# Merged gate lists carried to their sorting lanes by TensorE instead of four DMAs, with sort steps and first-tile gates moved between rounds

## The chip, the cores and the metric

The kernel runs on one core of a Trainium2 chip. The metric is the device time of the program in microseconds (us). The kernel before was run 9 times: median 312.01 us, lowest 308.48, highest 314.27. The engines are named as in the profile: PE is TensorE's matrix product, PEld its weight load, DVE is VectorE, ACT is ScalarE, POOL is GpSimd, SP is SyncE, which here only issues DMAs.

## What is computed

Two layers follow each other. The first is attention with a choice of key chunks; the second is a mixture of experts with a capacity.

```python
# attention: q, k, v are (4, 8, 768, 64); 24 chunks of 32 keys
ub = sum(max(q * k_min, q * k_max))            # bound of each chunk, for each query
top_chunks = argsort(where(causal, ub, -1e9))[..., -6:]
attn = softmax(scale * q @ k.T, only in the 6 chunks and causal)
x = (attn @ v) as (3072 tokens, 512)
# experts: 8 of them, each takes at most 80 tokens
expert = argmax(x @ w_gate); gate = its softmax weight
for e in range(8):
    tok = the 80 tokens of e with the highest gates
    out[tok] = gate[tok] * (relu(x[tok] @ w1[e]) @ w2[e])   # all other rows 0
```

So for each expert the 80 highest gates among 3072 tokens have to be known before the expert's tokens can be fetched.

## The kernel before

**Rounds.** The 32 pairs of batch and head are taken in eight groups of four (g = 0 to 7); two groups make a batch. The 768 queries of a group are three tiles of 256 (t = 0, 1, 2). A round `rd` is one pair of key blocks for one tile: a group has 1 + 2 + 3 = 6 rounds, and there are N = 48. Everything is in one hand-written order (`manual_schedule`): each engine runs its instructions in the order in which the Python code issues them, and waits only for semaphores.

**A round** issues, in this order: `rows` (for the tile that ended four rounds ago: TensorE transposes, L564, and the normalised rows of x by DVE, L565; at the second group of a batch the store of x to DRAM, L571), `scales` (tile that ended three rounds ago: L542, L544, L550, and in the second group of a batch `best`, which finds each token's expert, L581 to L603), `score` (L459, L463), `gate_rows` (L530, L534), `exps` (ACT, L474, four per round; on diagonal blocks a mask on POOL, L479), `sum_pairs` (POOL, L503), the queue `late` (`flush`), transposes of the next group's q and k on DVE (`step`, L262, L279), then `pace(rd)` **sort steps**, then the product with v for the round before (`value`, L492), its denominators (`denom`, L517), and in the round r = 3 of a group the bounds of the next group's chunks (`bound_all`, L390; `rank_all`, L402 to L410). At the end of the round stands `gates` (L616 to L640 on DVE): it turns a tile's winning logits into gates, writes them to `gmask`, and queues eight small POOL operations (`columns`, L623 to L650) that the next flush issues.

**The sort.** In a batch's second group, the gates of a tile go to `gmask`. Four generators then find the top 80 of each expert, eight at a time: one step is a MAX8 (L661) and a match-and-replace (L663) on DVE. `lanes1` sorts columns 0 to 7 of `gmask` in 64 lanes, `lanes_mid` merges them with columns 8 to 11 in 32 lanes, `lanes2` sorts columns 12 to 15 and merges (L703, result `M3`, 32 lanes of 80 values: four lists for each of eight experts). `lanes3` sorts what is left: two sets of eight lanes, at partitions 0 and 32, each with two of the four lists and one more column (16 or 17). To get there, `lanes2` moves the four lists by four DMAs from SBUF to SBUF on SP's queue (L707). Each generator starts with a TensorE transpose (`turned`, L669) into a PSUM tile of the pool `misc`, which has two buffers for all its tiles, and an ACT copy (`copied`, L674). Each list takes 10 steps. The generators run one after the other; `merges` holds them, and a generator is added three rounds after the round in which its tile ended. `pace(rd)` says how many steps a round issues; the step that ends a generator counts too.

**What needs the result.** In round 44 `freeze` transposes the eight thresholds to all partitions (L734, `ps_tau`), compares all gates with them (L745, L746), counts with TensorE (`ps_cum`, L755 to L759), and builds the old tokens' seats (L763 to L775, `ps_old`). It must be past the last sort step. `ps_tau` stands on TensorE's queue ahead of `value(43)`.

The steps of a round, and the end of `lanes2`:

```python
for _ in range(pace(rd)):
    if merges and next(merges[0], merges) is merges:
        merges.pop(0)
...
if 1 <= rd < N:
    value(rd - 1)
```

Of the kernel before, what the change touches and what calls it, by code (L numbers as in the profile page):

```python
# [8 lines left out]
F32 = mybir.dt.float32  # L9
# [12 lines left out]
NB = 4  # L22
# [3 lines left out]
NEXP = 8  # L26
DFF = 1024
CAP = 80
NPRE = 5
QBLK = SEQ // P  # L30
# [6 lines left out]
def kernel(  # L37
# [11 lines left out]
    nc = tc.nc  # L49
# [16 lines left out]
    ident_f32 = cpool.tile([P, P], F32, name="ident_f32")  # L66
# [136 lines left out]
    with tc.tile_pool(name="small", bufs=2) as small, \  # L203
# [11 lines left out]
        def misc(shape, dtype, name):  # L215
            return psM.tile(shape, dtype, space=bass.MemoryType.PSUM, tag="misc", name=name)
# [341 lines left out]
        def rows(g, t):  # L558
            b, gi = divmod(g, 2)
            npt, rec = nps.pop((g, t)), recs.pop((g, t))  # L560
            ps_xn = misc([P, 2, 2, P], F32, "ps_xn")
            for a in range(2):
                for j in range(2):
                    nc.tensor.transpose(ps_xn[:, j, a, :], npt[:, a, j * P:(j + 1) * P], ident_f32[:])  # L564
            nc.vector.tensor_tensor(  # L565
                out=xbuf[(b, t)][:, :, P * gi:P * (gi + 1)].bitcast(
                    BF16).rearrange("p j (k d) -> p j k d", d=HEAD_D),
                in0=ps_xn[:].rearrange("p j a (r d) -> p j (a r) d", d=HEAD_D),
                in1=rec[:, :, :, None].to_broadcast([P, 2, 4, HEAD_D]), op=ALU.mult)
            if gi == 1:  # L570
                nc.sync.dma_start(out=x_dram_v[:, QBLK * b + 2 * t:QBLK * b + 2 * t + 2, :],  # L571
                                  in_=xbuf[(b, t)][:])

        picked = {}

# [97 lines left out]
        def copied(dst, src):  # L673
            nc.scalar.activation(out=dst, in_=src, func=mybir.ActivationFunctionType.Copy)  # L674
# [17 lines left out]

        def lanes_mid():
            copied(S2[:, CAP:], turned(8, 4)[:])
            nc.gpsimd.memset(S3, -1.0)
            yield from sort_lanes(S2, L2)

        def lanes2():
            S, L = cand[0][32:64, 208:208 + P], cand[0][32:64, 416:416 + CAP]
            copied(S, turned(12, 4)[:])  # L700
            yield from sort_lanes(S, L)
            reversed_copy(back, L)
            nc.vector.tensor_tensor(out=M3, in0=L2, in1=back, op=ALU.max)  # L703
            yield
            for i in range(4):
                w, n = divmod(i, 2)
                nc.sync.dma_start(  # L707
                    out=cand[0][32 * n:32 * n + NEXP, 496 + CAP * w:496 + CAP * (w + 1)],
                    in_=cand[1][NEXP * i:NEXP * (i + 1), CAP:2 * CAP])

        def lanes3():
            for n in range(2):
# [298 lines left out]

        N = len(rounds)
        merges = []
        pace = lambda rd: {42: 6, 43: 6}.get(rd, ((0, 5, 3, 2, 1, 1), (0, 5, 1, 1, 1, 0))[rd // 6 % 2][rd % 6])
        steps_of = {1: ["K0"], 2: ["K1", "Q0"], 3: ["Q1"], 6: ["K0", "K1"], 7: ["Q0"], 8: ["Q1"]}
        for g in range(2, NQUAD - 1):
            steps_of.update({6 * g - 1: ["K0"], 6 * g: ["K1"], 6 * g + 1: ["Q0"], 6 * g + 2: ["Q1"]})
# [3 lines left out]
        with tc.manual_schedule(engines=set(mybir.EngineType) - {mybir.EngineType.Unassigned}):  # L1021
            first, others = slice(0, 2), slice(2, QBLK)
            load(0, k4, "kn", first)
            load(0, q4, "qn", first, nc.scalar)
            nc.scalar.activation(out=minus1[:], in_=crow[:], func=mybir.ActivationFunctionType.Exp,
                                 scale=1e-3)
            load(0, k4, "kn", others)
            load(0, q4, "qn", others)
            load_v(0, first)
            nc.sync.dma_start(out=wg_sb[:], in_=moe_w_gate.rearrange("(t r) e -> r t e", r=P))  # L1030
            load_v(0, others)
            load_k(1)
            load_q(1)
            load_v(1)
            idle(24)
            u = prep(0)
            units = [u]
            u["K"](0)
            u["Q"](0)
            flush()  # L1040
            u["bound"](1, 2)
            idle(5)
            u["K"](1)
            u["rank"](1, 2)
            u["Q"](1)
            build = {0: build_constants, 1: build_projection, 3: build_selection, 4: build_ties}
            for rd in range(N + 1):
                g, r = divmod(rd, 6)
                if r == 1 and 1 <= g < NQUAD - 1:
                    load_v(g + 1)  # L1050
                if r == (1 if g else 3) and g + 2 < NQUAD:
                    load_k(g + 2)
                if r == (3 if g else 4) and g + 2 < NQUAD:
                    load_q(g + 2)
                if 16 <= rd < 40 and rd % 2 == 0:
                    zero_fill((rd - 16) // 2)
                if rd - 4 in ends:
                    rows(*ends[rd - 4])
                if rd - 3 in ends:
                    eg, et = ends[rd - 3]  # L1060
                    scales(eg, et)
                ps_S = score(rd) if rd < N else None
                if rd - 2 in ends:
                    gate_rows(*ends[rd - 2])
                if rd < N:
                    exps(rd, ps_S)
                    if summed(rd):
                        sum_pairs(rd)
                flush()
                if rd - 3 in ends and eg == NQUAD - 1:  # L1070
                    gates(eg // 2, et)
                if rd in build:
                    build[rd]()
                if r in (2, 4) and 1 <= g <= NPRE or r == 2 and g == NPRE + 1:
                    load_whole(g - 1, r // 2 - 1)
                late_weights(rd)
                if rd == 0:
                    units[0]["bound"](2, 4)
                    units[0]["K"](2)
                    units[0]["rank"](2, 4)  # L1080
                    units[0]["Q"](2)
                elif rd == 1:
                    units[0]["bound"](4, 6)
                    units[0]["rank"](4, 6)
                for kind, f in steps_of.get(rd, []):
                    if (kind, f) == ("K", "0"):
                        units.append(prep(len(units)))
                    units[-1]["step"](kind, int(f))
                u = units[min(g + 1, NQUAD - 1)] if len(units) > g + 1 else None
                at = 3 if g else 4  # L1090
# [3 lines that stand above are left out]
                if (rd, 0) in frozen:  # L1094
                    next(fz, None)
                if rd == N - 1:
                    turn_new(0)
                if 1 <= rd < N:
                    value(rd - 1)
                    if r == at and g + 1 < NQUAD:  # L1100
                        u["bound_all"]()
                    if r == 5 and g + 1 < NQUAD:
                        u["unselect"]()
                    denom(rd - 1)
                    del Es[rd - 1]
                    gl, t, i, pr, n = rounds[rd - 1]
                    if i == n - 1:
                        evacuate(gl, t)
                        ends[rd - 1] = (gl, t)
                if r == at and g + 1 < NQUAD:  # L1110
                    u["rank_all"]()
                flush(bulk)
                if rd == N - 1:
                    weigh0()
                    turn_new(1)
                if (rd, 1) in frozen:
                    assert not merges
                    next(fz, None)
                if rd - 3 in ends:
                    eg, et = ends[rd - 3]  # L1120
                    if eg % 2 == 1 and eg < NQUAD - 1:
                        gates(eg // 2, et)
                    make = {(3, 0): lanes1, (3, 2): lanes_mid, (5, 1): lanes2, (5, 2): lanes3}.get(ends[rd - 3])
                    if make:
                        merges.append(make())
            last = (NQUAD - 1, 2)
            weigh1()
            denom(N - 1)
            value(N - 1)
            evacuate(*last)  # L1130
            weigh1_own()
            gate_rows(*last)
            held_back.pop(0)()
            scales(*last)
            held_back.pop(0)()
            weigh1_sum()
            gates(NB - 1, 2)
            flush()
            rows(*last)
            idle(10)  # L1140
            turn_new(2)
            weigh2()
# [108 lines left out]
```

## Time and profile before

| | |
|---|---|
| median of 9 runs | 312.01 us |
| the profiled execution | 313.38 us, of which the span from first to last instruction is 311.7 us |
| mean granted TensorE clock in it | 0.942 |
| PE busy | 265.0 us, 85% of the span |
| DVE busy | 201.4 us, 65% |
| ACT busy | 153.8 us, 49% |
| POOL busy | 196.5 us, 63% |
| the four DMAs of L707 | issued from 210.86 to 214.03 us |
| sort steps (L661, L663) on DVE | first at 120.7 us, last at 228.0 us |

A matmul line of the timeline merges many instructions, with the time from the first start to the last end. Square brackets at the end of a timeline line give how long the engine stood still before it and for whom; "issue" there means that the profile shows nobody that it waited for. PEclk is the clock that TensorE was granted, 1.00 being full speed; in the trace it is 1.00 or 0.50 in stretches of 3.4 us.

### The profile page before, as it was taken

Reading aid. Unit: us, or ns where it says so; the run is one execution under the profiler, and the core shown is the slowest. Engines: PE = TensorE matmul, PEld = TensorE weight load, DVE = VectorE, ACT = ScalarE, POOL = GpSimd, SP = SyncE. Lnnn points to the kernel's source line nnn. Section 1 sums busy time; section 2 is a strip of 40 time slices with the busy share of each in tenths; the row PEclk is TensorE's granted clock in tenths of the full one; section 3 lists DMA queues with packets and bytes.
Section 4 is the critical chain, followed back from the end, with each engine's and each line's share of the span. In section 5 each row is a group of like instructions: output and inputs, shape, how many; then the busy total and the mean of one; then the engine's idle time right before and its main releaser. Section 6 shows DMA issues by size and latency. Waiting matters only on the chain.

```text
span 311.7 us, 12157 instructions
## 1 busy us (share of the span) xinstructions
PE 265.0 (85%) x5018; PEld 158.8 (51%) x5018; DVE 201.4 (65%) x747; ACT 153.8 (49%) x351; POOL 196.5 (63%) x398
## 2 busy tenths in 40 slices
PE   8769789989979997989999798799556878779992
PEld 3326456546646664556666455455324544327760
DVE  4849279369747546998997597941868574742431
ACT  1643948727936863765686268526602334422120
POOL 8294886958967875896788579729913220237232
PEclk9999999999999999999999899979859589969998
DMA  7887706979999999999999996719998100102211
GB/s 173 173 181 147 147 3 140 191 148 171 200 220 247 212 252 267 208 211 234 274 205 248 270 214 184 130 44 137 201 208 136 36 3 34 34 23 67 63 59 40
DMA packets 59303, 47.80 MB, mean 153 GB/s; under 512 B 27910, under 2 KB 51590, under 8 KB 59248
## 3 DMA queue, kind: packets, MB, share of 16 engines
q1 hardware_dynamic: 45392, 28.10, 37.5%
q0 software_dynamic: 13536, 18.67, 34.7%
q8 instruction: 39, 0.64, 0.9%
q10 hardware_dynamic: 320, 0.26, 0.3%
q14 instruction: 16, 0.13, 0.1%
HBM read 53.10 MB, written 10.76 MB: 205 GB/s over the span
## 4 chain that ended last, share of the span: by engine, by line
PE 55%; DVE 18%; issue 11%; POOL 4%; DMA 4%; ACT 3%; SPq 2%; POOLq 1%; ACTq 0%; DVEq 0%
PE ps_num L492 21%; PE ps_den L517 8%; PE ps_u L390 7%; PE ps_S L459 6%; PE ps_xn L564 4%; PE ps_den L530 3%; DVE cand L663 3%; PE ps_S L463 2%; DVE cand L661 2%; POOL X L1154 2%; POOL out_dram L1196 2%; PE ps_dT L542 2%; DMA cand<-cand 2%; DVE cand L770 2%; ACT E L474 2%
## 5 line engine op out<-in xcount | busy, mean ns | idle before, releaser
L474 ACT ACTIVATE E<-ps_S 128x384 f32<-128x384 f32 (+1 forms) x192 | 88.7, 554 | 46.7 <-PE ps_S L463 46.7
L492 PE MATMUL ps_num<-E,vn 128*32 128x256 f32 (+1 forms) x1536 | 94.6, 366 | 3.3 <-issue 3.3
L503 POOL TENSOR_TENSOR both<-E 128x256 f32<-128x256 f32 x92 | 64.6, 732 | 23.3 <-ACT E L474 23.2
L492 PEld LDWEIGHTS ps_num<-E,vn 128*32 128x32 f32 x1536 | 50.8, 112 | 34.0 <-issue 10.8
L479 POOL TENSOR_SCALAR_AFFINE_SELECT E<-E 128x256 f32<-128x256 f32 x96 | 41.4, 461 | 34.3 <-ACT E L474 34.3
L459 PE MATMUL ps_S<-QB,KB 32*128 32x256 bf16 (+1 forms) x768 | 35.4, 264 | 2.4 <-ACT E L474 1.7
L534 ACT ACTIVATE DSB<-ps_den 128x256 f32<-128x256 f32 x24 | 9.2, 385 | 42.3 <-PE ps_den L530 38.7
L463 PE MATMUL ps_S<-PENT,ind 32*128 32x256 bf16 (+1 forms) x384 | 25.1, 258 | 2.5 <-DVE PENT L377 2.5
L517 PE MATMUL ps_den<-E,ones 128*32 128x256 f32 (+1 forms) x400 | 23.4, 339 | 2.2 <-issue 2.2
L459 PEld LDWEIGHTS <-KB 32*128 32x128 bf16 x768 | 17.2, 94 | 15.2 <-issue 11.9
L287 POOL CAST KB<-kT 128x768 bf16<-128x768 f32 (+1 forms) x18 | 24.1, 1343 | 0.0
L565 DVE TENSOR_TENSOR x_nat<-ps_xn,rec 128x512 bf16<-128x512 f32 x24 | 16.5, 686 | 11.2 <-PE ps_xn L564 8.1
L517 PE MATMUL ps_den<-both,ones 128*32 128x256 f32 x184 | 19.5, 402 | 0.0
L402 DVE STREAM_TRANSPOSE ub<-ps_u 128x160 f32<-128x160 f32 x28 | 7.4, 318 | 18.6 <-PE ps_u L390 18.6
L296 ACT ACTIVATE qp<-qT 128x640 f32<-128x640 f32 (+2 forms) x20 | 12.8, 647 | 12.4 <-DVE qT L262 12.3
L517 PEld LDWEIGHTS ps_den<-E,ones 128*32 128x32 f32 x400 | 13.2, 112 | 10.8 <-issue 5.9
L661 DVE MAX8 cand<-cand 64x8 f32<-64x128 f32 (+3 forms) x40 | 13.7, 342 | 6.9 <-DMA cand<-cand 4.2
L262 DVE STREAM_TRANSPOSE kT<-kn 128x768 f32<-128x768 f32 (+1 forms) x17 | 15.6, 919 | 3.7 <-DMA kn<-in_k_dram 3.6
L564 PE MATMUL ps_xn<-ident_f,npt 128*128 128x128 f32 x96 | 16.6, 298 | 1.6 <-DVE sm L616 1.0
L523 ACT ACTIVATE npt<-ps_num 128x512 f32<-128x512 f32 x24 | 14.8, 616 | 5.0 <-PE ps_num L492 5.0
L279 DVE TENSOR_REDUCE KMM<-kT 128x24 f32<-128x768 f32 (+1 forms) x20 | 15.8, 791 | 1.5 <-PE ps_u L355 0.9
L1196 POOL DMA_INDIRECT out_dram<-Y,sidx x8 | 7.4, 922 | 13.9 <-DVE Y L1194 13.9
(238 smaller groups left out, 459.2 us busy)
## 6 DMA issues: line engine op xcount, KB each, us to landing
w<-in_moe_w_dram POOLq DMA_DIRECT2D x11, 1024.0 KB, 10.8
out_dram<-zero_tile SPq DMA_DIRECT2D x12, 512.0 KB, 12.3
kn<-in_k_dram SPq DMA_DIRECT2D x28, 192.0 KB, 5.0
qn<-in_q_dram SPq DMA_DIRECT2D x28, 192.0 KB, 7.0
vn<-in_v_dram SPq DMA_DIRECT2D x28, 192.0 KB, 5.2
x_dram<-x_nat SPq DMA_DIRECT2D x12, 257.0 KB, 5.5
kn<-in_moe_w_dram POOLq DMA_DIRECT2D x1, 768.0 KB, 7.9
qn<-in_moe_w_dram POOLq DMA_DIRECT2D x1, 768.0 KB, 12.6
```

What stands on the lines that cost most here:

```text
L287: nc.gpsimd.tensor_copy(out=straight(KB[s][:, f, ts]), in_=natural(kT[:, f, ts]))
L390: nc.tensor.matmul(out=tiles[h][32 * j:32 * (j + 1), :, :], lhsT=KMM[s][rs, w, f, :], rhs=x[rs, j], start=(w == 0 and f == 0), stop=(w == ...
L459: nc.tensor.matmul(out=ps_S[h][:, m, 0:wid], lhsT=KB[s][rs, w, keys], rhs=QB[s][rs, w, q0:q0 + wid], start=(w == 0), stop=False, skip_grou ...
L463: nc.tensor.matmul(out=ps_S[h][:, m, lo - q0:wid], lhsT=ind[rs, keys], rhs=PENT[s][rs, lo - NFULL:q0 + wid - NFULL], start=False, stop=Tru ...
L474: nc.scalar.activation(out=E[:].rearrange("p m q -> p (m q)")[:, 0:last], in_=ps_S[h][:].rearrange("p m q -> p (m q)")[:, 0:last], func=my ...
L479: nc.gpsimd.affine_select(out=diag, in_=diag, compare_op=ALU.is_ge, fill=0.0, base=0, pattern=[[0, 2], [1, 4], [4, CHUNK]], channel_multip ...
L492: nc.tensor.matmul(out=NUM[q0:q0 + 32, a, c0:THIRD], lhsT=nats[(g, "vn")][:, kb, 2 * a + r, 32 * f:32 * (f + 1)], rhs=Es[rd][2 * a + r][:, ...
L503: nc.gpsimd.tensor_tensor(out=both[:], in0=E[:, 0, :], in1=E[:, 1, :], op=ALU.add)
L517: nc.tensor.matmul(out=dn[32 * h:32 * (h + 1), c0:THIRD], lhsT=ones32[:], rhs=src, start=(i == 0 and m == 0), stop=False, skip_group_check ...
L564: nc.tensor.transpose(ps_xn[:, j, a, :], npt[:, a, j * P:(j + 1) * P], ident_f32[:])
L565: nc.vector.tensor_tensor(out=xbuf[(b, t)][:, :, P * gi:P * (gi + 1)].bitcast(BF16).rearrange("p j (k d) -> p j k d", d=HEAD_D), in0=ps_xn ...
L661: nc.vector.max(out=top, in_=src)
```

## The change

Four edits. (1) `lanes2` ends with four TensorE products with shifted 32 columns of the identity instead of four DMAs; they write the four lists to a PSUM tile `ps_m` of pool `misc` at partitions 0 and 32, and one ACT copy of 40x160 brings them to the lanes of `lanes3`. The POOL memset of those lanes shrinks to the columns that are not copied. (2) For the first tile of a group (t = 0) the gates, and with them the start of `lanes1`, come four rounds after its end instead of three: from the end of round 6g+3, behind `rank_all`, to the end of round 6g+4. (3) Since the stored rows hold the gate, the store of x for such a tile moves behind its gates (except in the last batch). (4) `pace` is set anew.

```diff
-            if gi == 1:
-                nc.sync.dma_start(out=x_dram_v[:, QBLK * b + 2 * t:QBLK * b + 2 * t + 2, :],
-                                  in_=xbuf[(b, t)][:])
+            if gi == 1 and (t or b == NB - 1):
+                store(b, t)
+
+        def store(b, t):
+            nc.sync.dma_start(out=x_dram_v[:, QBLK * b + 2 * t:QBLK * b + 2 * t + 2, :],
+                              in_=xbuf[(b, t)][:])
...
         def lanes_mid():
             copied(S2[:, CAP:], turned(8, 4)[:])
-            nc.gpsimd.memset(S3, -1.0)
+            nc.gpsimd.memset(S3[:, 2 * CAP:], -1.0)
...
             nc.vector.tensor_tensor(out=M3, in0=L2, in1=back, op=ALU.max)
             yield
+            ps_m = misc([64, 2 * CAP], F32, "ps_m")
             for i in range(4):
                 w, n = divmod(i, 2)
-                nc.sync.dma_start(
-                    out=cand[0][32 * n:32 * n + NEXP, 496 + CAP * w:496 + CAP * (w + 1)],
-                    in_=cand[1][NEXP * i:NEXP * (i + 1), CAP:2 * CAP])
+                nc.tensor.matmul(out=ps_m[32 * n:32 * (n + 1), CAP * w:CAP * (w + 1)],
+                                 lhsT=ident_f32[0:32, NEXP * i:NEXP * i + 32], rhs=M3, start=True, stop=True,
+                                 skip_group_check=True)
+            copied(S3[:, 0:2 * CAP], ps_m[0:40, :])
...
-        pace = lambda rd: {42: 6, 43: 6}.get(rd, ((0, 5, 3, 2, 1, 1), (0, 5, 1, 1, 1, 0))[rd // 6 % 2][rd % 6])
+        pace = lambda rd: {23: 1, 40: 3, 41: 4, 42: 4, 43: 4}.get(
+            rd, ((0, 4, 1, 3, 0, 1), (0, 4, 4, 3, 0, 1))[rd // 6 % 2][rd % 6])
...
-                if rd - 3 in ends:
-                    eg, et = ends[rd - 3]
-                    if eg % 2 == 1 and eg < NQUAD - 1:
+                for d in (3, 4):
+                    eg, et = ends.get(rd - d, (0, 0))
+                    if eg % 2 == 1 and eg < NQUAD - 1 and (et == 0) == (d == 4):
                         gates(eg // 2, et)
-                    make = {(3, 0): lanes1, (3, 2): lanes_mid, (5, 1): lanes2, (5, 2): lanes3}.get(ends[rd - 3])
-                    if make:
-                        merges.append(make())
+                        if et == 0:
+                            store(eg // 2, et)
+                        make = {(3, 0): lanes1, (3, 2): lanes_mid, (5, 1): lanes2,
+                                (5, 2): lanes3}.get((eg, et))
+                        if make:
+                            merges.append(make())
```

Counted out, the steps fall like this (the step that ends a generator included; rounds without a step left out):

| rounds | before | after |
|---|---|---|
| 22 to 27 | 1 in 22, then 5, 3, 2 in 25 to 27 | 1 in 23, then 4, 1, 3 in 25 to 27 |
| 28 to 35 | 1, 1 in 28 and 29; 5, 1, 1, 1 in 31 to 34 | 1 in 29; 4, 4, 3 in 31 to 33; 1 in 35 |
| 37 to 40 | 5, 3, 2, 1 | 4, 1, 3, 3 |
| 41 to 43 | 1, 6, 6 | 4, 4, 4 |

`M3` is ready with the step of round 41 before, and with the last step of round 40 after. The move to the lanes of `lanes3` is the first step of round 42 before, and the first step of round 41 after.

## Prediction

> **What bounds the kernel now.** I read the wait view first, for TensorE: who stood still longest, and for whom. From the answer sorted by time:
>
> ```profile
> PE ps_tau L734 <- DVE cand L717: 7.2, 1, 7.2
> ...
> DVE cand L661 <- DMA cand<-cand: 4.2, 1, 4.2
> ```
>
> The columns are total us, times, longest. TensorE's longest wait in the run is the threshold transpose of round 44, which waits for the end of the last sort. The sort in turn waited for the four DMAs. The timeline of each engine gives the times. DVE, SP and TensorE:
>
> ```profile
> 210.56 0.23 DVE L703 TENSOR_TENSOR cand<-cand,cand 32x80 f32<-32x80 f32 x1
> ...
> 218.67 0.45 DVE L661 MAX8 cand<-cand 40x8 f32<-40x288 f32 x1 [4.16 <-DMA cand<-cand]
> ```
> ```profile
> 210.86 3.17 SPq L707 DMA_DIRECT2D cand<-cand  x4
> ```
> ```profile
> 221.48 0.63 PE L530 MATMUL ps_den<-npt,wgx 128*32 128x256 f32 x4
> 229.27 0.27 PE L734 MATMUL ps_tau<-ident_f,cand 8*128 8x8 f32 x1 [7.16 <-DVE cand L717]
> 229.47 3.64 PE L492 MATMUL ps_num<-E,vn 128*32 128x256 f32 x32
> 232.88 1.08 PE L517 MATMUL ps_den<-both,ones 128*32 128x256 f32 x8
> ```
>
> M3 is ready at 210.79, its lanes only at 218.67: 3.17 us of issue, then 5.14 us (in the chain of waits) until the last transfer lands. Ten steps follow without a gap to 229.21. So the chain is DVE, SP, DMA, DVE, and TensorE stands. The last two lines show a second cost: 32 products take 3.64 us, where the same line takes 1.93 at 214.77. The windows view says why (columns: PE, PEld, DVE, ACT, POOL busy, PEclk, DMA share, GB/s):
>
> ```profile
> 118.50:121.90 3.40, 1.89 (x32) 1.07 (x36) 2.59 (x12) 1.88 (x6) 2.56 (x9) 1.00 1.08 256
> ...
> 173.10:176.50 3.40, 1.41 (x28) 0.78 (x22) 2.39 (x12) 1.78 (x5) 2.47 (x8) 1.00 1.10 248
> 176.50:179.90 3.40, 3.40 (x46) 1.48 (x42) 1.19 (x6) 0.00 (x0) 1.85 (x6) 0.50 1.07 328
> ...
> 229.30:234.50 5.20, 5.20 (x45) 2.35 (x46) 1.91 (x6) 0.00 (x0) 0.00 (x0) 0.50 1.16 208
> ```
>
> After stretches in which TensorE was busy 35 to 43% (1.18 of 3.40 at 200.4, 1.41 at 173.1) the next 3.4 us were granted half speed; after one at 56% (1.89 at 118.5) they were not. A half stretch full of work costs 1.7 us.
>
> **Edit 1 with the new steps of rounds 40 to 43.** Removed: four DMAs, whose path from M3 to the first step is 7.88 us. Added: four products, a copy, and an earlier place. DVE has room in round 40: it stands 3.73 us ahead of L544 at 209.80. Its three steps there (0.70, a lone MAX8 of 0.28, then L684 and L703 of 0.53) take about 1.5 us from 205.79, so M3 is ready near 207.3. The four products come in round 41 behind `score`, at 210.46, and wait for nothing. No row has this form; the two transposes of L669 at 214.21 take 0.63 together, so four small ones lie between 0.3 and 1.3, and I take 0.45, nearest to that row.
>
> Now a new wait. TensorE's queue then holds the transposes of columns 16 and 17 and `value(40)`. `misc` has two buffers: the second transpose takes the buffer of `ps_m`, which the ACT copy must empty. That copy is queued behind the four exponentials of round 41 (210.62 to 212.68 on ACT). Copies of the L674 rows take 0.27, so: copy to 212.95, second transpose 213.0 to 213.3, its copy to 213.6, first step of the last sort near **213.7 instead of 218.67**. TensorE stands from 211.2 to 213.0, 1.8 us, and `value(40)` with all behind it starts at 213.3 instead of 210.46: 2.84 later, less 0.56 because the transposes no longer stand in round 42 (214.21 to 214.77). So TensorE comes to `ps_tau` at 222.11 + 2.28 = 224.4.
>
> DVE's last sort is 218.67 to 229.21, 10.54 us, now cut by the x row of round 42 (0.61): 213.7 + 10.54 + 0.61 = 224.85. Both arrive nearly together; `ps_tau` runs near 225.0 instead of 229.27, **4.3 earlier**.
>
> **The clock behind it.** TensorE no longer stands 7 us, so `value(43)` and its denominators run at full speed: 3.64 - 1.93 and 1.08 - 0.61 are 2.18, of which the overlap of the two lines leaves 2.1. That stays on the path: DVE ends its scan at 231.31 and then waits 3.40 for `ps_cum`, that is for these products, and from there to `ps_old` (6.1 us of DVE work, TensorE waiting 2.92) nothing else is in between. **2.1 earlier.** Against it, the new 1.8 us wait in round 41 makes its stretch 47% busy, between the 43 and 56% above. Half speed after it would cost TensorE 1.7, of which 0.45 is hidden behind DVE's later arrival: 1.2. I take half, **0.6 later**; the ends are 0 and 1.2.
>
> The Trainium skill, "TensorE: Matmul & The Clock Gate", section "HAM oscillation — how this bites in real kernels", has a milder rule: only idle gaps over about 3.4 us bring the clock down. By it the new wait costs no clock, and the sum would be 0.6 better. This trace halves after gaps of 1.99 and 2.22 us, so the rows decide. On the DMAs, "DMA: Bandwidth & Descriptors", "Anatomy of one DMA — SWDGE (gpsimd) path", gives a fixed cost near 2 us for a transfer; by that the lanes could have been ready near 215.5 and edit 1 would be worth some 3 us less. The trace has 5.14, and I go by it.
>
> **Edit 2, first-tile gates.** In round 22 the transpose of `lanes1` waits 1.87 us for `gmask` (118.14 to 120.01), since the gates stand behind the ranking. In the new order it comes in round 23, when the gates are long done. I still give it **0**. The same places of the cycle 12 rounds earlier and later, without that transpose, show TensorE standing for nobody: 1.34 at 65.27 and 1.99 at 173.78. In each case the trace's instruction queue (39 packets of 16 KB) starts a packet about 1 us ahead or less (64.28, 173.40), and one starts at 118.97 too. So the wait for `gmask` probably covers a wait for instructions. The ends: 1.9 gained; or 0 gained and a half stretch as at 176.5, 1.7 lost. The gates' `columns` on POOL come one round later, behind L503 and ahead of the key cast and the mask of round 24: up to 0.6 on `value(24)`, which the 1.37 us wait of round 27 for DVE takes up.
>
> **Steps of rounds 23 to 39.** 0.7 us (64x128 or 32x128) or 0.86 us (32x208) each. Rounds 22 to 27 hold 11 before and 9 after. DVE is full from 123.24 to 139.5, where TensorE waits 1.37 us for it; before that point it runs five of these steps in either order (five in round 25; one in 23 and four in 25): nothing. Rounds 31 to 35 are shifted most: the first transpose of `lanes_mid` moves into round 31, where DVE must wait for an ACT copy behind the exponentials (to 161.1), about 3 us of standing; then 4 + 3 steps put the ranking of round 33 at about 174 to 178 instead of 170.4 to 174.0. Its reader on TensorE, the transpose of round 35, is at 181.29, and DVE's own next work at 178.54 waited 2.94 us for TensorE. So it is hidden with about 1 to 3 us left; if TensorE's 1.99 us stop at 173.78 were gone, 1 to 2 us of it would show. Round 39's ranking comes after one full step less. Sum **0**, ends -0.7 and +2.
>
> **Edit 3 and the memset.** The store of x is the next issue on SP's queue in the same round, 0.7 us later; behind it stand a zero fill and the loads of a group needed ten rounds on. POOL's memset takes 0.36 and shrinks. Nothing reads either early: 0. In the last batch both are unchanged.
>
> **The sum.** 4.3 + 2.1 - 0.6 + 0 + 0 = **5.8 us**. The profiled execution took 313.38 us for a span of 311.7; it should come to 307.6. It lies 1.4 above the median of 312.01, inside the runs' own 308.48 to 314.27; 5.8 off the median gives **306.2 us**.
>
> **Rivals.**
>
> (a) The round 22 wait goes without a substitute and the clock stays up: 5.8 + 1.9 + 0.6 = 8.3, 303.7 us. For it: no packet shows a stop at every place. One half stretch less behind `ps_old`, 1.7, would make 302.0, my lower end.
>
> (b) Covered waits appear. The instruction packet at 220.75 starts while TensorE is about to stand 7 us; uncovered it costs 1.3 to 2.2 as the other stops do, and a half stretch 1.7: 5.8 - 3.7 = 2.1 left, 309.9 us. For it: DMA is over full there (share 1.13 to 1.24).
>
> (c) The change does not do what it says: M3 comes no earlier, because DVE reaches round 40 later than 207 by the steps moved to 37 to 40, and the last sort begins past 217. Then 1 to 1.5 us are left, 311 us. Against it: the 3.73 us that DVE stands there.
>
> (d) Slower. TensorE's 1.8 us wait in round 41 brings the clock down, and short waits (`ps_tau`, then 2.9 at `ps_old`) keep it down. Between 214 and 248 the trace has ten stretches of 3.4 us, five of them already at half. Each further one costs 1.7; four eat the 6.4 us of the two gains, and all five give 8.5 - 6.4 = 2.1 slower, 314.1 us. Against it: a stretch at 56% busy kept full speed.
>
> **How the numbers follow.** About 0.5% (1.6 us) is what a measurement of this kernel can tell from no change. Forecast 0.57, (a) 0.14, (b) 0.14, (c) 0.08, (d) 0.07. Faster: the forecast, (a) and nearly all of (b), 0.83; same: (c) and the rest of (b), 0.10; slower: (d), 0.07. The range goes from 302.0 to 311.0: (a) with its bound, (b), and half of (c).
>
> **What would show it.** `ps_m` in round 41 with M3 done 3 us before; the second L669-type transpose of round 41 waiting about 1.8 us for ACT; the first 40x288 MAX8 about 3.3 us after `score(41)` ends, with no DMA in between; TensorE's wait at `ps_tau` under 1 us; `value(43)` in about 1.9 us at clock 1.00; in round 22 either no stop or one of "issue". I am wrong if TensorE still stands over 3 us at `ps_tau`, if `value(43)` runs at half speed, or if a new wait of over 2 us stands in rounds 31 to 35.

## The result and the profile after

The changed kernel took **304.78 us** (median of 20 runs, 301.13 to 307.44); the kernel before, run beside it, 311.33 us (62 runs, 307.7 to 318.15). The ratio is **0.9798, interval 0.9769 to 0.9828**: 6.3 us less, between 5.4 and 7.2. The prediction was 5.8. The profiled execution took 303.3 us with a span of 301.6, at a mean granted clock of 0.959. Ratios here leave out executions over 1.5% above the fastest of their kernel, so they are not always the quotient of the medians.

The wait view of the changed kernel, TensorE from 108 to 260 us (total us, times, longest):

```profile
PE ps_old L780 <- DVE x_nat L565: 2.9, 1, 2.9
...
PE ps_g L672 <- ACT cand L677: 1.6, 1, 1.6
...
PE ps_S L459 <- DVE ub L402: 1.2, 1, 1.2
PE ps_num L492 <- issue: 1.2, 1, 1.2
...
PE ps_tau L739 <- DVE cand L722: 0.6, 1, 0.6
```

The wait at `ps_tau` has gone from 7.2 to 0.6 us. A new one of 1.6 stands at `ps_g` (the second transpose of round 41), and one of 1.2 at the scores of round 34. The timeline of DVE, then of TensorE (the four products are eight instructions there):

```profile
205.97 0.23 DVE L706 TENSOR_TENSOR cand<-cand,cand 32x80 f32<-32x80 f32 x1
209.29 0.45 DVE L664 MAX8 cand<-cand 40x8 f32<-40x288 f32 x1 [2.72 <-ACT cand L677]
...
213.56 0.69 DVE L565 TENSOR_TENSOR x_nat<-ps_xn,rec 128x512 bf16<-128x512 f32 x1 [1.20 <-issue]
```
```profile
206.26 0.47 PE L711 MATMUL ps_m<-cand,ident_f 32*32 32x80 f32 x8
206.72 0.27 PE L672 MATMUL ps_g<-ident_f,gmask 128*8 128x128 f32 x1
208.58 0.38 PE L672 MATMUL ps_g<-ident_f,gmask 128*8 128x128 f32 x1 [1.59 <-ACT cand L677]
208.89 2.79 PE L492 MATMUL ps_num<-E,vn 128*32 128x256 f32 x32
...
221.84 0.22 PE L739 MATMUL ps_tau<-ident_f,cand 8*128 8x8 f32 x1 [0.56 <-DVE cand L722]
221.99 1.93 PE L492 MATMUL ps_num<-E,vn 128*32 128x256 f32 x32
223.74 0.61 PE L517 MATMUL ps_den<-both,ones 128*32 128x256 f32 x8
```

`M3` ends at 206.20 and the last sort begins 3.1 us later; it was 7.9. `value(43)`, the second last line, is back at 1.93 us from 3.64. But `value(40)` behind the new wait takes 2.79 us instead of 1.51, at half clock. The transposes of round 42's x row stand behind it on TensorE, so that row (L565) comes late too, and the sort, which has it in its middle on DVE's queue, stands 1.20 us there.

The two profiled executions differ by 10.1 us of span, more than the medians do. To tell the change from what comes and goes, I cut each trace at two places: **A** is from the start to the end of `denom(39)`, the last denominators of round 40; **B** from there to the end of `value(43)`; **C** the rest. Each cut is a start plus a duration from TensorE's timeline (before: 208.62 + 0.78 = 209.40, and 229.47 + 3.64 = 233.11).

| first profile of | A | B | C |
|---|---|---|---|
| before | 209.4 | 23.7 | 78.6 |
| after | 205.1 | 18.8 | 77.7 |

So 10.1 is 4.3 in A, 4.9 in B and 0.9 in C. In A the profile of before holds two stops of TensorE for nobody, 1.99 at 173.78 (round 34) and 2.22 at 200.89 (round 39), each followed by a half-speed stretch. A second profile of the same code (e8) has the first with 1.61 and the second with 0.65, and no half speed behind either; the experiments will show that A wanders. B is the change. C's 0.9 is small against what profiles with the same code behind that point differ by (77.6 in f1 and 79.0 in f2).

### The profile page after: what moved, and what is told of

The parts are those of the page before. It is cut to its first block, busy times and chain, and to the rows that moved or that the text cites. A ratio compares the mean times of both kernels' runs of the same rounds, so it can differ in the third digit from the quotient of the medians.

```text
span 301.6 us, 12164 instructions
## 1 busy us (share of the span) xinstructions
PE 265.7 (88%) x5026; PEld 158.0 (52%) x5026; DVE 200.8 (67%) x747; ACT 154.3 (51%) x352; POOL 197.0 (65%) x398
## 4 chain that ended last, share of the span: by engine, by line
PE 51%; DVE 22%; issue 11%; POOL 7%; ACT 5%; DMA 2%; POOLq 1%; DVEq 0%; ACTq 0%
PE ps_num L492 18%; PE ps_den L517 6%; PE ps_S L459 6%; PE ps_u L390 6%; DVE cand L666 3%; ACT E L474 3%; PE ps_den L530 3%; DVE cand L664 3%; PE ps_xn L564 3%; PE ps_num L918 3%; DMA x_dram<-x_nat 2%; PE ps_S L463 2%; POOL X L1163 2%; POOL out_dram L1205 2%; DVE cand L775 2%
## 5 line engine op out<-in xcount | busy, mean ns | idle before, releaser
L492 PE MATMUL ps_num<-E,vn 128*32 128x256 f32 (+1 forms) x1536 | 95.6, 366 | 3.2 <-issue 2.8
L479 POOL TENSOR_SCALAR_AFFINE_SELECT E<-E 128x256 f32<-128x256 f32 x96 | 42.4, 469 | 34.6 <-ACT E L474 34.6
L459 PEld LDWEIGHTS <-KB 32*128 32x128 bf16 x768 | 17.2, 94 | 16.2 <-issue 13.0
L565 DVE TENSOR_TENSOR x_nat<-ps_xn,rec 128x512 bf16<-128x512 f32 x24 | 16.4, 685 | 9.2 <-PE ps_xn L564 5.0
L402 DVE STREAM_TRANSPOSE ub<-ps_u 128x160 f32<-128x160 f32 x28 | 7.4, 316 | 17.8 <-PE ps_u L390 17.8
L517 PE MATMUL ps_den<-both,ones 128*32 128x256 f32 x184 | 19.2, 380 | 0.0
L262 DVE STREAM_TRANSPOSE kT<-kn 128x768 f32<-128x768 f32 (+1 forms) x17 | 15.6, 919 | 4.0 <-DMA kn<-in_k_dram 3.6
```

What stands on the lines that cost most here:

```text
L459: nc.tensor.matmul(out=ps_S[h][:, m, 0:wid], lhsT=KB[s][rs, w, keys], rhs=QB[s][rs, w, q0:q0 + wid], start=(w == 0), stop=False, skip_grou ...
L479: nc.gpsimd.affine_select(out=diag, in_=diag, compare_op=ALU.is_ge, fill=0.0, base=0, pattern=[[0, 2], [1, 4], [4, CHUNK]], channel_multip ...
L492: nc.tensor.matmul(out=NUM[q0:q0 + 32, a, c0:THIRD], lhsT=nats[(g, "vn")][:, kb, 2 * a + r, 32 * f:32 * (f + 1)], rhs=Es[rd][2 * a + r][:, ...
L517: nc.tensor.matmul(out=dn[32 * h:32 * (h + 1), c0:THIRD], lhsT=ones32[:], rhs=src, start=(i == 0 and m == 0), stop=False, skip_group_check ...
L565: nc.vector.tensor_tensor(out=xbuf[(b, t)][:, :, P * gi:P * (gi + 1)].bitcast(BF16).rearrange("p j (k d) -> p j k d", d=HEAD_D), in0=ps_xn ...
```

## The experiments

One chip, here the first, ran e1 to e4 (kernel before: median 312.85 of 35 runs), a second e5 to e8 (319.62, 11 runs), a third f1 to f4 (311.58, 17 runs). A, B and C of every profile:

| kernel (chip) | A | B | C | ratio of the time to before, interval |
|---|---|---|---|---|
| e8 before (2nd) | 207.1 | 23.0 | 86.1 | |
| e1 after, with the DMAs (1st) | 207.7 | 24.0 | 79.0 | 0.9959, 0.9909 to 1.0009 |
| e2 before, with edit 1 (1st) | 206.5 | 21.9 | 78.3 | 0.9952, 0.9905 to 0.9999 |
| e3 before, with edits 2 and 3 (1st) | 205.2 | 23.2 | 78.5 | 1.0023, 0.9980 to 1.0067 |
| e4 before, wait filled (1st) | 204.4 | 21.8 | 77.6 | 1.0002, 0.9943 to 1.0062 |
| f4 the same (3rd) | 206.1 | 21.8 | 77.4 | 0.9932, 0.9884 to 0.9981 |
| e7 after (2nd) | 206.0 | 19.0 | 85.7 | |
| f1 after (3rd) | 204.1 | 17.4 | 77.6 | 0.9782, 0.9717 to 0.9847 |
| e5 after, one tile (2nd) | 209.5 | 17.2 | 87.1 | 0.9763, 0.9698 to 0.9827 |
| f2 the same (3rd) | 206.5 | 17.2 | 79.0 | 0.9753, 0.9687 to 0.9820 |
| e6 one tile, second wait filled (2nd) | 205.6 | 17.1 | 84.4 | 0.9739, 0.9680 to 0.9799 |
| f3 the same (3rd) | 204.7 | 17.1 | 77.4 | 0.9707, 0.9641 to 0.9773 |

A lies between 204.1 and 209.5 with no order by kernel; B falls into groups that follow the edits. C is 7 to 8 us longer on the second chip in all four profiles (see the end).

**e1: the changed kernel with the four DMAs back.** The new steps and the late gates stay.

```diff
-            nc.gpsimd.memset(S3[:, 2 * CAP:], -1.0)
+            nc.gpsimd.memset(S3, -1.0)
...
-            (ps_m, its four products, its copy)
+            for i in range(4):
+                w, n = divmod(i, 2)
+                nc.sync.dma_start(
+                    out=cand[0][32 * n:32 * n + NEXP, 496 + CAP * w:496 + CAP * (w + 1)],
+                    in_=cand[1][NEXP * i:NEXP * (i + 1), CAP:2 * CAP])
```

> The changed kernel with the four DMAs put back in place of the products and the copy; gates, store and steps stay as changed. My theory (the transport and the place where it stands make the gain together): M3 is ready at 206.2 as in the changed kernel, the DMA path takes about 7.9 us, so the last sort begins near 214.1 instead of 209.3 and ends near 225.5. TensorE does not stand in round 41, reaches ps_tau 3 us earlier than in the changed kernel and stands about 7 us there, and the clock falls behind it. Time: 5 to 6 us slower than the changed kernel, 0 to 1.5 us faster than the kernel before. Rival (the new distribution of the steps makes the gain, the transport is hidden): 4 us or more faster than the kernel before.

Its last sort, on DVE's timeline, and its threshold, on TensorE's:

```profile
216.95 0.45 DVE L664 MAX8 cand<-cand 40x8 f32<-40x288 f32 x1 [7.80 <-DMA cand<-cand]
```
```profile
228.03 0.27 PE L737 MATMUL ps_tau<-ident_f,cand 8*128 8x8 f32 x1 [6.88 <-DVE cand L720]
228.22 3.44 PE L492 MATMUL ps_num<-E,vn 128*32 128x256 f32 x32
```

`M3` ends at 208.77, the last sort begins at 216.95: 8.2 us, and B is as long as before. The median is 310.20; the ratio leaves 0 to 3 us for the rest of the change; the theory had 0 to 1.5. Without edit 1 the wait and the half speed behind it are both there.

**e2: the kernel before with edit 1 alone.** The reverse diff, applied to before; the steps stay old, so `M3` comes in round 41 and its products in round 42.

> The kernel before with edit 1 alone (products and copy for the four DMAs, smaller memset); old steps, old gates. My theory: M3 is ready in round 41 as before, the move is the first step of round 42, behind score(42) on TensorE and behind the exponentials of round 42 on ACT, so the last sort begins near 217.0 instead of 218.7, TensorE stands about 1.4 us for the copy in round 42 and about 3 us at ps_tau; two half-speed stretches behind it instead of three. Time: 2 to 3.5 us faster than the kernel before. Rival (the DMAs' own latency is the whole gain, steps do not matter): 5 us or more faster.

TensorE, then DVE:

```profile
211.35 0.47 PE L708 MATMUL ps_m<-cand,ident_f 32*32 32x80 f32 x8
...
224.64 0.27 PE L736 MATMUL ps_tau<-ident_f,cand 8*128 8x8 f32 x1 [3.75 <-DVE cand L719]
224.84 3.64 PE L492 MATMUL ps_num<-E,vn 128*32 128x256 f32 x32
```
```profile
213.96 0.45 DVE L661 MAX8 cand<-cand 40x8 f32<-40x288 f32 x1 [2.31 <-ACT cand L674]
```

`M3` ends at 207.94, the products stand in TensorE's order at 211.35, and the ACT copy stands behind the exponentials of that round: 6.0 us in all, where the DMAs took 7.2 (e8) to 8.2 (e1) and the full change 3.1. B falls by 1.1 to 1.8 us (23.0 and 23.7 less 21.9), and `value(43)` stays at half speed, since 3.75 us of wait are left. The ratio says 1.5 us, between 0 and 3, less than the 2 to 3.5 expected; the medians are 4.0 apart (308.89 and 312.85). So **the parts do not add up**: in B, edit 1 without the new steps gains 1 to 2 us, the steps without edit 1 nothing (24.0), both together 4 to 6.

**e3: the kernel before with the gates and the store of the first tile a round later.** As in the diff of the change; the steps of rounds 22 and 23 are exchanged.

```diff
+        pace = lambda rd: {22: 0, 23: 1, 42: 6, 43: 6}.get(...)
```

> The kernel before with the first tile's gates and store one round later, and the one step of round 22 in round 23; all else as before. My theory: the 1.9 us for gmask in round 22 goes, and TensorE stands about 1.3 to 2 us for nobody (issue) in value(21) instead: 0 within 0.7 us. Rival (the wait for gmask was a cost of its own): 1.9 us faster, and no stop in round 22.

TensorE in round 22:

```profile
120.40 1.07 PE L492 MATMUL ps_num<-E,vn 128*32 128x256 f32 x16 [1.53 <-issue]
122.96 0.30 PE L672 MATMUL ps_g<-ident_f,gmask 128*64 128x128 f32 x1
```

The transpose waits for nobody now, but `value(21)` stops in its middle for 1.53 us with no releaser. All nine profiles with this edit show that stop, 1.23 to 2.15 us; none of the five without it does, which have the wait of 1.9 us for `gmask`. The ratio of 1.0023 (0.9980 to 1.0067) leaves no room for 1.9 us gained: the wait covered another one, as predicted. The last section shows what the other one is.

**e4 and f4: the kernel before with 28 idle products in the wait.** They are added work that nobody reads.

```diff
+            ps_fill = wide("ps_fill")
+            for _ in range(28):
+                nc.tensor.matmul(out=ps_fill[:], lhsT=ident_bf[:], rhs=ties[:, 0:4 * P], start=True, stop=True)
             (ps_tau follows)
```

> The kernel before with 28 products of 128x512 into a spare PSUM tile ahead of ps_tau, whose result nobody reads: TensorE works while it waits for the last sort. My theory: ps_tau runs at the same time as before, the clock stays at 1.00, value(43) takes 1.9 us instead of 3.6: 2.1 us faster than the kernel before. Rival (value(43) is slow for another reason, such as operands that come late): value(43) stays near 3.6 us and the time is the same.

> Kernel before with 28 idle products in the wait ahead of the threshold; the lists still come by DMA and the last sort starts no earlier. Theory (half speed of value(43) and of its denominators costs 2.1 us on the path): ratio 0.993, value(43) in 1.9 us. Rival (what this stretch gains is given back by later waits, or the added instructions cost as much): ratio 1.000 with value(43) in 1.9 us all the same, and a later stretch that is longer by 2 us.

TensorE in e4:

```profile
217.97 6.20 PE L735 MATMUL ps_fill<-ties,ident_bf 128*128 128x512 bf16 x28 [0.86 <-ACT E L474]
224.11 0.22 PE L738 MATMUL ps_tau<-ident_f,cand 8*128 8x8 f32 x1
224.26 1.93 PE L492 MATMUL ps_num<-E,vn 128*32 128x256 f32 x32
```

`value(43)` runs in 1.93 us with the lists still moved by DMA: it was the idle time ahead of it that halved the clock. B is 1.2 to 1.9 us shorter than before in both profiles and C about 1.0, so the longer later stretch of the rival is not there. The times agree less well: 1.0002 in e4, 0.9932 in f4. Weighted by their intervals that is 0.996 plus or minus 0.004, so 1.2 us plus or minus 1.2. The mechanism is shown, its 2.1 us in the time are not contradicted and not confirmed.

**e5 and f2: the changed kernel without the new wait.** Both columns are turned into one tile of `misc`, so the second transpose needs no buffer that ACT has to empty.

```diff
+            ps_g = misc([NEXP, 2, P], F32, "ps_g")
             for n in range(2):
-                copied(cand[0][32 * n:32 * n + NEXP, 496 + 160:496 + 288], turned(16 + n, 1)[:])
+                nc.tensor.transpose(ps_g[:, n, :], gmask[:, 16 + n, :], ident_f32[:])
+            for n in range(2):
+                copied(cand[0][32 * n:32 * n + NEXP, 496 + 160:496 + 288], ps_g[:, n, :])
```

> The changed kernel with the transposes of columns 16 and 17 in one PSUM tile instead of two: the second no longer takes the buffer that ps_m holds. My theory: the 1.6 us wait of round 41 for the ACT copy goes, and the half-speed stretch behind it; TensorE reaches ps_tau some 3 us earlier and stands there for the sort, which begins only 0.3 us earlier but no longer waits 1.2 us for the x row of round 42: 1 to 1.7 us faster than the changed kernel, ps_tau wait 1.5 to 2.5 us. Rival (the last sort alone sets the time and TensorE's wait in round 41 costs nothing): the same time within 0.5 us.

> Changed kernel with both transposes of columns 16 and 17 in one PSUM tile, so that the second waits for no copy. Theory (the new wait and the half-speed stretch behind it cost 0.6 to 1.8 us on the path): 0.6 to 1.8 us below the changed kernel on this chip, ratio to the kernel before 0.974 to 0.978. Rival (the wait is hidden behind the last sort, which sets the time of the threshold either way): within 0.5 us of the changed kernel.

TensorE in f2; the first line is both transposes with no wait:

```profile
208.08 0.38 PE L719 MATMUL ps_g<-ident_f,gmask 128*8 128x128 f32 x2
208.39 1.51 PE L492 MATMUL ps_num<-E,vn 128*32 128x256 f32 x32
...
221.60 0.22 PE L742 MATMUL ps_tau<-ident_f,cand 8*128 8x8 f32 x1 [1.72 <-DVE cand L725]
```

The wait is gone, and `value(40)` takes 1.51 us in all four profiles of this version. Against f1, where the wait was there and the clock stayed up all the same, B gains only 0.2 (17.4 to 17.2): TensorE reaches `ps_tau` earlier and waits 1.72 us for the sort instead of 0.56. So the wait itself is hidden; what it can cost is the clock behind it. In the time theory and rival are not to be told apart: 303.76 and 303.60 are the medians of f2 and f1.

**e6 and f3: the same, with 12 idle products ahead of `ps_old`.** The edit of e4, at another place; the trace has records of 11 of the 12 products.

> The kernel of e5 with 12 products of 128x512 into a spare PSUM tile ahead of ps_old, nobody reads them: they fill the 2.9 us for which TensorE waits there. My theory: the two half-speed stretches behind ps_old (6.8 us) go, and about 2 to 3 us with them, against e5. Rival (that part waits for DVE anyway): the same as e5 within 0.7 us.

> The same with 12 idle products ahead of the first products of the second threshold pass; they compute nothing that is used. Theory (the 2.9 us wait there brings the clock to half for 6.8 to 10.2 us, on the path): 1.5 to 2.5 us below the kernel with one tile alone. Rival (the stretch behind it is bound by VectorE and ScalarE, so that TensorE's clock there is covered): within 0.7 us of it.

TensorE in f3:

```profile
226.35 2.76 PE L783 MATMUL ps_fill<-ties,ident_bf 128*128 128x512 bf16 x11
229.35 0.83 PE L787 MATMUL ps_old<-slotrhs,cand 128*80 128x48 bf16 x18 [0.23 <-DVE x_nat L565]
```

The changed kernel has 6.8 us of half speed right behind this wait (from 232.2; in f1 from 229.6). In f3 it is 3.4 (from 232.1), and in e6 the first comes at 242.3; but f2, without the products, has only 3.4 there too (from 233.3). Both medians lie 2.7 us under those of e5 and f2 (310.27 to 312.98, 301.06 to 303.76), and C falls by 2.7 and 1.6, as the theory has it. But C of f3 is only 0.2 below that of f1, whose code there is that of f2, and the intervals overlap. It is the fastest version tried, at 0.9707; that it beats the changed kernel is likely and not settled.

**e7, e8 and f1: both kernels once more.**

> The changed kernel once more, unchanged, for a second profile. My theory: the stops of TensorE for nobody (issue) in rounds 10, 15, 22, 34 and 39 come and go between executions, each with 1.2 to 2.2 us; the waits for ACT in round 41 (1.6 us) and at ps_tau (0.6) come again within 0.4 us. Rival: the stops stand where they stood in the first profile (round 22 alone).

> The kernel before once more, unchanged, for a second profile. My theory: 7 us again at ps_tau and three half-speed stretches behind it; the stops for nobody stand elsewhere or are of another number than the four of the first profile. Rival: the same four stops (rounds 10, 15, 34 and 39), so that they belong to the kernel before and the change removed two of them.

> The changed kernel itself, as the yardstick for the other three on this chip. From the last denominators of round 39 to the end of value(43) its profiles took 18.8 to 19.0 us, those of the kernel before 23.0 to 23.7. Theory (the path through the last sort is what the change shortens): 0.980 of the kernel before, 6 us less, of which 4 to 5 us lie in that stretch. Rival (most of the 10 us between the first two profiled executions is real): below 0.972.

f1 gives 303.60 and 0.9782: the result repeats on the third chip (0.980 was expected). B of the changed kernel is 18.8, 19.0 and 17.4; e8 puts before at 23.0. The 1.5 us between f1 and the other two are the half-speed stretch behind the new wait. The windows of e7 (columns as in the prediction), then of f1, each with the stretch that holds the wait and the next:

```profile
206.10:209.50 3.40, 1.78 (x36) 0.94 (x35) 1.23 (x7) 2.28 (x6) 3.26 (x5) 1.00 0.34 27
209.50:212.90 3.40, 3.40 (x38) 1.87 (x38) 2.55 (x9) 0.34 (x2) 3.40 (x6) 0.51 1.17 186
```
```profile
205.70:209.10 3.40, 1.78 (x35) 1.04 (x34) 0.87 (x3) 2.24 (x7) 3.39 (x5) 1.00 0.83 99
209.10:212.50 3.40, 3.40 (x77) 2.17 (x73) 3.23 (x11) 1.50 (x4) 2.60 (x5) 1.00 1.20 190
```

TensorE was busy 1.78 us of 3.40 in both; the next stretch got 0.51 in one and 1.00 in the other.

The stops for nobody did not come and go as I had expected of e7 and e8; the rivals were nearer. e7 has its stops of over 1 us in rounds 10, 15 and 22, like the first profile of after. e8 has them in rounds 10, 15 and 34, like before, and the one of round 39 shrank to 0.65. Round 34 in before, in e8 and in after:

```profile
175.77 1.26 PE L492 MATMUL ps_num<-E,vn 128*32 128x256 f32 x16 [1.99 <-issue]
```
```profile
178.05 1.07 PE L492 MATMUL ps_num<-E,vn 128*32 128x256 f32 x16 [1.61 <-issue]
```
```profile
174.24 1.07 PE L459 MATMUL ps_S<-QB,KB 32*128 32x256 bf16 x8 [1.24 <-DVE ub L402]
```

All six profiles with the old steps have that stop (1.15 to 1.99 us). Of the eight with the new steps six have the wait of the last line instead (0.87 to 1.51) and two a stop (0.75 in e6, 1.43 in f2). The rest of e7 and e8 came as expected, but for two half-speed stretches behind the wait at `ps_tau` of e8 (6.5 us) where I had put three.

## Why the prediction was right

**Edit 1 with the new steps, 4.3 earlier: right, and by the mechanism named.** Counted from the end of `denom(39)`, the first step of the last sort was put at 4.3 us (213.7 less 209.40) and came at 4.1 to 4.2 in the three profiles of the changed kernel; `ps_tau` was put at 15.6 and came at 15.3 in f1 and at 16.8 and 16.9 where the clock halved. The two profiles of before have it at 19.9 and 19.2, so it came 3.8 to 4.5 us earlier with the clock up and 2.3 to 3.1 with it halved. The products took 0.47 us, put at 0.45; the new wait is 1.6 us, put at 1.8, at the place and for the copy named. e1 and e2 show that the products and their earlier place are both needed.

One part of that step was wrong: `M3` was to be ready 3 us before its products. It ends 0.06 us before they start (206.20 and 206.26). I read the room from DVE's standing in round 40 of the one profiled execution. Before, then e8:

```profile
209.80 0.21 DVE L544 RECIPROCAL rec<-ps_dT 128x8 f32<-128x8 f32 x1 [3.73 <-PE ps_dT L542]
```
```profile
207.47 0.21 DVE L544 RECIPROCAL rec<-ps_dT 128x8 f32<-128x8 f32 x1 [0.79 <-PE ps_dT L542]
```

In before TensorE had just lost 2.22 us to a stop and more to a half-speed stretch, and DVE stood for that; in e8 it waits 0.79 us. Counted from `denom(39)`, `M3` ends at 1.1 us in the three profiles of the changed kernel and at 1.4 in both of before: a round earlier in the order moved it by 0.3 us. What the new steps bought is the products' place in round 41 instead of 42. That `M3` was there in time was luck, and there is no reserve: a later `M3` would hold TensorE. No run has the products in round 41 with the old steps, so how much of the new steps that place needs stays open.

Two smaller readings: the 3.17 us of issue and the 5.14 until landing overlap by 0.62, as the 5.14 starts at 213.41, inside the issue; the sum used the whole path of 7.88 and stands. And the section on DMAs that the prediction names is, by its title, on transfers issued by GpSimd, while SyncE issued these four; the prediction did not go by its figure.

**The clock behind the wait, 2.1 earlier: right in kind.** `value(43)` and its denominators take 1.93 and 0.61 us in all profiles of the changed kernel, and e4 gets the same by idle products alone. In B and C of e4 and f4 that is 2 to 3 us; in their time it is 1.2 plus or minus 1.2.

**Half speed behind the new wait, 0.6 later: the size was off.** It is no average cost but a draw: 0 in f1, 1.4 to 1.6 in the other two (B). The prediction took 0.45 of it as hidden behind DVE. The profile of after shows why it is not: the late products delay the x row of round 42, which DVE has to write in the middle of the sort (the 1.20 us there). The bound was drawn too narrowly too: I put it between 43 and 56% busy; 52% went either way, and in the first profile of after 61% (2.06 of 3.40 us from 204.9 to 208.3) was followed by half speed.

**Round 22, 0: right**, and for the reason given; e3 and all nine profiles show the wait for instructions in place of the one for `gmask`.

**Steps of rounds 23 to 39, 0: right in the sum.** What the prediction had as its condition came, though at another place. It looked at the transpose of round 35 as the ranking's reader; but the scores of round 34 take the PSUM tiles that the ranking's first instruction (L402) has to empty, and they wait for it, 1.24 us (1.51 in e7, 0.87 in f1). That wait stands where the old steps have the stop of 1.15 to 1.99 us: one took the place of the other, as in round 22. The waits at `ps_dT` fell from 2.7 to 1.3 us. A does not tell the kernels apart.

**The sum.** 5.8 was put against 6.3 measured (5.4 to 7.2). B and C of the changed kernel together lie 5.8 us under those of before in the first two profiles and 4.4 in e7 and e8; what is left of the 6.3 no profile places. Rival (b), a stop uncovered near 220 us, did not come: in the seven profiles with all four edits TensorE has no stop for nobody of over 0.3 us from 200 to 240 us. (c) was nearer than I thought, by the 0.06 us; (d) needed four more half stretches of 3.4 us between 214 and 248 us than the five that before had: after has two there.

## What to carry to other kernels

Moving a small result between partitions through TensorE paid in full only where the product and its copy also stood early in their engines' orders: the path from the result to the first step of the sort went from 7.2 to 8.2 us to 6.0 with the products alone, and to 3.1 with their place in the round before. When a wait ahead of TensorE goes, look whether the trace has half speed behind it, and count that as a second gain. A new wait of 1.6 us cost here either nothing or one half-speed stretch, so give it both prices. Read slack from several executions: the room seen in one may be the trace of another engine's stop. And where a wait disappears and the time does not, look for the one that it covered.

## What the runs showed of the hardware

**Half speed follows short waits, but not always.** Waits of 1.6 us were followed by a half-speed stretch in two profiles of the changed kernel and not in the third, at the same busy share. The Trainium skill, "TensorE: Matmul & The Clock Gate", section "HAM oscillation — how this bites in real kernels", names idle gaps over about 3.4 us as the cause; these are less than half of that. Cut into the trace's own stretches of 3.41 us, the fourteen profiles have 771 at full speed from 55 to 255 us. Where TensorE was busy under 44% of one, the next was at half speed in all 28 cases; from 44 to 64% in 8 of 62; above 64% in none of 681 (there is one at 66%, behind 255 us in before). What decides between 44 and 64% is open. It is not alone where in the stretch the wait lies: in e7 it ended as the next stretch began, and half speed followed; but in e7 from 172.00, too, where the wait came first and TensorE worked to the end (1.95 of 3.41 us), and it did not in e8 from 87.60 (1.57 of 3.41), where TensorE stood over the end.

**A stop of one chip.** All four profiles on the second chip have, in the last stage, a wait that the other ten lack. TensorE's waits in e7 from 255 to 300 us:

```profile
PE ps_H L1186 <- ACT XT L1175: 6.7, 2, 6.1
```

In the other profiles it is 1.3 in all. On the second chip the longest is 6.1 to 7.2 us in both kernels and their variants, and the median of the kernel before there is 319.62 against 312.85 and 311.58. It stands in both kernels, and its cause is open; it is why kernels are compared on one chip only.

**Waits for instructions keep their place, and other waits cover them.** Every profile has a stop of 1.3 to 2.4 us in the products that start near 67 us, and one of 0.3 to 2.5 near 91; those of rounds 22 and 34 follow the edits, as told above; the one of round 39 is 0.5 to 2.2 in five of the six profiles with the old steps and in none of the others. That the stops in `value` of rounds 10, 22 and 34 are waits for instructions can be read from the traces, though no run tested it: there are 31 of over 0.7 us, from 0.75 to 2.35 long, and each ends 2.2 to 2.5 us after a 16 KB packet of the instruction queue started. A packet that starts 0.05 us before the stop goes with 2.15 us, one that starts 1.68 before it with 0.75. Where TensorE had waited for something else shortly before, as for `gmask` in round 22, it comes to the same place 2.2 to 3.3 us after the packet, and there is no stop.
